# Retention and mixture of experts on one core: another order for the first two pairs of chunks

## The chip, the core and the metric

The kernel runs on one core of a Trainium2 chip. The metric is the device time of one execution in microseconds (us), lower is better; a kernel's time is the median of several executions. Times inside the kernel are read from a profile of one execution, in us from the start of its span.

## What is computed

The input is q, k and v of 4 batches, 8 heads, 768 positions and 64 channels, all float32. Each head keeps a state that decays by its own factor gamma; the output of that stage becomes the tokens of a layer with 8 experts, of which each token uses one.

```python
for t in range(S):
    state = gamma[None, :, None, None] * state + einsum('bhd,bhe->bhde', k[:, :, t], v[:, :, t])
    y[:, :, t] = scale * einsum('bhd,bhde->bhe', q[:, :, t], state)
...
x = y.transpose(0, 2, 1, 3).reshape(B * S, H * D)
logits = x @ w_gate
expert_idx = argmax(logits, axis=1)
...
    h = maximum(xe @ w1[e], 0.0)
    out[mask] = gate_w[mask, None] * (h @ w2[e])
```

## The kernel before, in words

The first stage goes over 24 chunks of 128 positions (all 8 heads of one batch at once, 6 chunks to a batch), two chunks to a turn of the loop over `k`: in turn `k`, `a` is chunk 2k and `b` is chunk 2k+1. The instructions stand in the order in which the code is written, on each engine by itself; nothing rearranges them. Later stages run the experts; the change does not touch them.

A chunk's input is one tile `qkv_t` of 128 partitions and four blocks: q and k turned (block 0 and 1, channels on the partitions), v and k as they are (blocks 2 and 3). `load(g, part)` fetches blocks of chunk g with one DMA issued on SyncE's queue (SP); all four blocks are 1,024 KB, two are 512 KB. Five such buffers go round, and `vs0`, the scaled v of chunk 0, lies in the first of them, so that the load of chunk 4 waits until chunk 0's `vs0` is used up.

For a chunk g the work is:

- `scale(g)`: v times a decay by position, into `vs` (line 250; GpSimd for all chunks but chunk 0, which VectorE does before the change).
- `scores(g)`: q times k on TensorE into two PSUM tiles `sp` (line 261), then VectorE multiplies them with the masked decay `M` into `Sb` (line 264, two instructions).
- `update(g)`: k times `vs` added into the running state `U` in PSUM (line 275), then ScalarE copies it scaled into one of three `ub` tiles (line 280, four instructions).
- `carry(g)`: the state of the chunks before, `ub` of chunk g-1, times q, into `Y` (line 291); the first chunk of a batch has none.
- `output(g)`: `Sb` times v, added into `Y` (line 302). `turn_out(g)`: VectorE multiplies `Y` with the decay `G` into `xT` (line 310).
- `gate_rows` turns a pair's output into rows and gate logits (lines 333, 317, 343).

`G` is made by one TensorE matmul `spread` from the small tile `g2` (the input `gdec`, two rows of 640) and a ScalarE copy. `cs` holds constants; its first part, which `M` needs, is loaded first. Ahead of all of this TensorE runs `WARM` matmuls of ones into the PSUM tile `warm`, which nothing reads.

Of the kernel before, what the change touches and what calls it, by code (L numbers as in the profile page):

```python
# [9 lines left out]
F32 = mybir.dt.float32  # L10
# [8 lines left out]
E, DM, F = 8, 512, 1024  # L19
N = B * S  # L20
P = 128
NP = H // 2
C = 128
# [20 lines left out]
IDS = 0x3FFF  # L44
FILLED = 160
ZROWS = 96
WARM = 12
FILL = (2, 2, 2, 2)
AHEAD = 5
BIG = 1 << 20  # L50
# [62 lines left out]
def retention_moe(ctx, tc, qkv, wts, cst, gdec, out):  # L113
    nc = tc.nc
# [44 lines left out]
    ones = gate.tile([P, P], BF16, name="ones")  # L159
# [51 lines left out]
    with ExitStack() as actx:  # L211
# [8 lines left out]
        ps_m = apool("ps_m", 1, space=PS)  # L220
# [3 lines left out]
        G = flat[:, 0:NP * C].rearrange("p (n t) -> p n t", n=NP)  # L224
# [12 lines left out]
        def load(g, part=slice(0, 4)):  # L237
            if g not in qs:
                qs[g] = ld.tile([P, 4, DM], F32, name="qkv_t", tag="ld")
            nc.sync.dma_start(out=qs[g][:, part], in_=qkv[g][:, part])  # L240
# [51 lines left out]
                                             rhs=q[half[r], p, :], start=(first and m == 0), stop=False,  # L292
                                             skip_group_check=True)

        def output(g):
            Y, Sb = Ys[g], Sbs[g]
            vp = qs[g][:, 2].rearrange("a (n d) -> a n d", n=NP)
            for m in range(2):
                for r in range(2):
                    for o in range(2):  # L300
                        p = 2 * m + o
                        nc.tensor.matmul(out=Y[half[o], r, m * C:(m + 1) * C], lhsT=vp[:, p, half[r]],  # L302
                                         rhs=Sb[:, r, p, :], start=False, stop=True, skip_group_check=True)

        def turn_out(g):
            Y = Ys[g]
# [147 lines left out]
        g2 = rawp.tile([2, DM + P], F32, name="g2", tag="raw")  # L454
        vs0 = ld.tile([P, H, D], F32, name="vs0", tag="ld")

        qs[1], qs[0] = [ld.tile([P, 4, DM], F32, name="qkv_t", tag="ld") for _ in range(2)]
        nc.sync.dma_start(out=cs[:, 0:NFIRST], in_=cst[:, 0:NFIRST])
        load(0)
        load(1, slice(0, 2))  # L460
        load(1, slice(2, 4))
        nc.sync.dma_start(out=g2, in_=gdec)
        nc.vector.memset(run, 0.0)
        nc.gpsimd.memset(meta0, 0.0)
        nc.scalar.copy(out=top, in_=run[:, 0:1])
        nc.vector.memset(wgs, 0.0)
        nc.vector.memset(zeros, 0.0)
        warm = ps_m.tile([P, 512], F32, name="warm", tag="mm")
        for i in range(WARM):
            nc.tensor.matmul(out=warm, lhsT=ones, rhs=ones.unsqueeze(1).broadcast_to([P, 4, P]), start=True, stop=True)  # L470
        load(2)
        load(3, slice(0, 2))
        load(3, slice(2, 4))
# [1 line left out]
        for r in range(2):  # L475
            nc.vector.tensor_tensor(
                out=M[:, r], in0=causal.unsqueeze(1).broadcast_to([P, NP, C]), op=ALU.mult,
                in1=cv[:, 0].rearrange("a (n t) -> a t n", t=2)[:, r].unsqueeze(2).broadcast_to([P, NP, C]))
        scale(0, nc.vector, vs0)
        scores(0)  # L480
        update(0)
        load(4)
        stages = {}
# [20 lines left out]
        for k in range(NCH // 2):  # L504
            a, b = 2 * k, 2 * k + 1
            batch, c = divmod(a, CPB)
            last = k == NCH // 2 - 1
            if k:
                scores(a)
            scores(b)  # L510
            carry(a, True)
            carry(b, c == 0)
            if last:
                xt0 = ld.tile([P, KD, EARLY], F32, name="xt0", tag="ld")
                for j, w in HALVES:
                    turn_slices(nc, xt0, xg0, j, w)
            if k - 1 in CHOSEN:
                stages["advance"]()
                if not last:
                    stages["weights"]()  # L520
            sends = list(range(*SENDS.get(k, (0, 0))))
            scale(b)
            if k not in (4, NCH // 2 - 1) and sends:
                send_x(sends.pop(0))
            if not last:
                scale(b + 1)
            if k == 10:
                send_x(sends.pop(0))
            for j, i in enumerate(SPLITS.get(k, ())):
                split(0, *divmod(i, 4), nc.gpsimd if j and k < 10 else nc.vector, 1)  # L530
            if k > 1:
                gate_rows(k, sends)
            if k == 1:
                nc.vector.tensor_tensor(out=us, in0=causal, in1=ident, op=ALU.subtract)
                nc.vector.tensor_scalar(out=run, in0=k_("ebase"), scalar1=1.0 / P, scalar2=None, op0=ALU.mult)
                for to, n in ((0, E), (E, 1)):
                    nc.vector.tensor_copy(out=wgs[:, :, to:to + n],
                                          in_=k_("gate").rearrange("p (n e) -> p n e", e=E)[:, :, 0:n])
            if k == 0:
                output(a)  # L540
            if c < CPB - 2:
                update(b)
            if not last:
                for i in sends:
                    send_x(i)
            if last:
                hidden, low, result, send, hidden_early = early_half(tc, ring[:, 4:6].rearrange("a j q m -> a j (q m)")[:, :, 0:DM],
                                            wk.tile([P, 4, EARLY], F32, name="rx0", tag="xT"),
                                            ps_1.tile([P, EARLY], F32, name="ph0", tag="U"),
                                            wp, ps_s, wparts, xhl, sidx0, meta0, out)  # L550
            if k in CHOSEN:
                stages = gating(CHOSEN[k])
                stages["choose"]()
                stages["soft"]()
            if last:

                after(EA[0:1, GROUPS[-2][0], 1:2])
                nc.gpsimd.tensor_tensor(out=xhl[:, 1], in0=xt0, in1=xhl[:, 0].bitcast(F32), op=ALU.subtract)
                for i in sends:
                    send_x(i)  # L560
            if k:
                output(a)
            output(b)
            if k == 0:
                spread = ps_m.tile([P, NP, C], F32, name="spread", tag="mm")
                nc.tensor.matmul(out=spread, lhsT=g2[:, DM:], rhs=g2[:, 0:DM], start=True, stop=True)
                nc.scalar.copy(out=G, in_=spread)
            turn_out(a)
            turn_out(b)
            if k == 1:  # L570
                gate_rows(k)
            if not last:
                update(b + 1)
            if k in CHOSEN and not last:
                stages["rank"](ps_m, "mm")
                stages["slots"]()
                if k == NCH // 2 - 2:
                    stages["weights"]()
            for g in range(2 * k + AHEAD, min(2 * k + AHEAD + 2, NCH)):
                load(g, slice(0, 4 if g % CPB < CPB - 1 else 3))  # L580
            if k == 1:
                for e in (E, E9):
                    clear(slice(e * N + FILLED, e * N + FILLED + ZROWS))
            if k in FETCHES:
                fetch(0, FETCHES[k])
            if k == 9:
                xg0 = ring[:, 2 * CPB - 2:].rearrange("a g q m -> a (g q) m")
                xhl = new_xhl(EARLY)
                load_x(xg0, E9, NJ0)
                load_meta(meta0[:, 0:2], E9, 2)  # L590
# [617 lines left out]
```

## Time and profile before

| | |
|---|---|
| time, median of 3 executions | 389.41 us (388.25 to 389.46) |
| the profiled execution | 388.81 us, of which the profile's span is 387.0 us |
| TensorE busy | 377.4 us, 98% of the span |
| VectorE, ScalarE, GpSimd busy | 258.6, 153.8, 164.1 us |
| HBM read and written | 65.07 and 15.19 MB |

A row of the timeline gives the start, how long the row's instructions took together, the engine, the line, the operation, the tile written and the tiles read, and their count; in brackets stands how long the engine had been idle and what ended that. PE is TensorE's matmul side, PEld its weight load, DVE is VectorE, ACT ScalarE, POOL GpSimd, SPq the queue of SyncE. Matmuls overlap at their ends, so the work of a row is read from its start to the next row's start, where no wait lies between. A float32 matmul of the code is two instructions in the trace.

### The profile page before, as it was taken

To read this page: it belongs to the slowest core of one execution; us is meant where nothing else is said; L and a number is where in the kernel's file an instruction comes from. 1 tells how busy PE (TensorE), PEld (TensorE's weight loads), DVE (VectorE), ACT (ScalarE), POOL (GpSimd) and SP (SyncE) were. 2 spreads that over 40 slices of the span, in tenths; PEclk is the share of its full clock that TensorE was granted. 3 is DMA by queue.
4 is the path that set the end of the run, shared out by engine and by line. 5 is a ranking of instruction groups with operands and counts; after the bars stand their busy time and mean duration, and the time that the engine had idled before them with its cause. 6 is when DMAs were issued, how large, how long until landed. Compare 5 with 4: busy or idle time off the path is not lost.

```text
span 387.0 us, 8716 instructions
## 1 busy us (share of the span) xinstructions
PE 377.4 (98%) x3279; PEld 353.3 (91%) x3279; DVE 258.6 (67%) x566; ACT 153.8 (40%) x315; POOL 164.1 (42%) x154
## 2 busy tenths in 40 slices
PE   7999999999999999899999999999999999999994
PEld 4888888888989899799999999999999999999984
DVE  4547759789878687656784777387747847776411
ACT  2335455454634455324530553155234406423200
POOL 0332755848721241001742383347317523732743
PEclk9999999999999999999999999999999999999999
DMA  7999799997358589781658357635836683530111
GB/s 274 416 382 345 275 417 420 406 383 238 141 152 209 187 278 221 244 205 30 239 167 205 101 180 193 173 132 163 226 122 197 224 205 127 183 113 5 57 42 58
DMA packets 30207, 80.65 MB, mean 208 GB/s; under 512 B 4811, under 2 KB 18767, under 8 KB 23732
## 3 DMA queue, kind: packets, MB, share of 16 engines
q1 hardware_dynamic: 24868, 66.87, 53.3%
q0 software_dynamic: 5264, 12.69, 9.1%
q8 instruction: 58, 0.95, 1.0%
q14 instruction: 17, 0.14, 0.1%
HBM read 65.07 MB, written 15.19 MB: 207 GB/s over the span
## 4 chain that ended last, share of the span: by engine, by line
PE 93%; DMA 3%; POOL 1%; SPq 1%; issue 1%; DVE 0%; POOLq 0%; DVEq 0%
PE ph L993 34%; PE py L1039 27%; PE py L1037 6%; PE sp L261 5%; PE Y L302 5%; PE xp L317 3%; DMA qkv_t<-qkv 3%; PE ph L775 3%; PE Y L291 2%; PE U L275 2%; PE L L333 2%; PE ph L915 1%; PE py L793 1%; PE lp L343 1%; POOL vs L250 1%
## 5 line engine op out<-in xcount | busy, mean ns | idle before, releaser
L733 POOL DMA_INDIRECT out<-Z,sidx x82 | 93.9, 1145 | 133.0 <-DVE Z L932 109.3
L150 DVE TENSOR_TENSOR wlo<-raw,whi 128x1024 fp32r<-128x1024 f32 (+1 forms) x67 | 75.7, 1134 | 8.2 <-ACT whi L148 7.1
L148 ACT CAST whi<-raw 128x1024 fp32r<-128x1024 f32 (+1 forms) x72 | 67.5, 952 | 1.3 <-DMA raw<-w 1.3
L1039 PE MATMUL py<-hh,whi 128*128 128x392 f32 (+4 forms) x192 | 66.3, 345 | 1.4 <-issue 1.3
L1005 ACT ACTIVATE hh<-ph 128x64 fp32r<-128x64 f32 (+7 forms) x72 | 32.3, 460 | 87.6 <-PE ph L993 86.2
L1039 PE MATMUL py<-hl,whi 128*128 128x392 f32 (+4 forms) x192 | 66.1, 344 | 0.0
L1039 PE MATMUL py<-hh,wlo 128*128 128x392 f32 (+4 forms) x192 | 66.0, 344 | 0.0
L1007 DVE SCALAR_TENSOR_TENSOR hl<-ph,hh 128x64 fp32r<-128x64 f32 (+7 forms) x72 | 36.4, 515 | 32.9 <-ACT hh L1005 32.0
L993 PE MATMUL ph<-xh,whi 128*128 128x392 f32 (+5 forms) x224 | 49.3, 342 | 0.0
L993 PE MATMUL ph<-xh,wlo 128*128 128x392 f32 (+5 forms) x224 | 49.0, 340 | 0.0
L993 PE MATMUL ph<-xl,whi 128*128 128x392 f32 (+5 forms) x224 | 49.0, 340 | 0.0
L993 PEld LDWEIGHTS ph<-xh,whi 128*128 128x128 f32 x224 | 40.3, 188 | 0.4
L993 PEld LDWEIGHTS ph<-xh,wlo 128*128 128x128 f32 x224 | 40.4, 188 | 0.2
L993 PEld LDWEIGHTS ph<-xl,whi 128*128 128x128 f32 x224 | 40.2, 188 | 0.2
L752 ACT CAST xh<-xt 128x512 fp32r<-128x512 f32 (+7 forms) x27 | 14.9, 552 | 61.6 <-DVE xt L743 61.6
L1039 PEld LDWEIGHTS py<-hh,whi 128*128 128x128 f32 x192 | 36.1, 188 | 2.2 <-issue 2.0
L1039 PEld LDWEIGHTS py<-hl,whi 128*128 128x128 f32 x192 | 36.2, 188 | 0.3
L1039 PEld LDWEIGHTS py<-hh,wlo 128*128 128x128 f32 x192 | 36.1, 188 | 0.2
L250 POOL TENSOR_TENSOR vs<-qkv_t,cs 128x512 f32<-128x512 f32 x19 | 19.8, 1044 | 36.9 <-DMA qkv_t<-qkv 31.5
L264 DVE TENSOR_TENSOR Sb<-sp,xgs 128x512 f32<-128x512 f32 x48 | 29.9, 682 | 4.4 <-PE sp L261 4.4
L733 POOL DMA_INDIRECT xs_dram<-xn,KEY x24 | 25.5, 1063 | 12.5 <-PE lp L343 4.9
L280 ACT ACTIVATE ub<-U,cs 128x64 f32<-128x64 f32 x80 | 18.5, 314 | 24.7 <-PE U L275 24.7
(169 smaller groups left out, 524.2 us busy)
## 6 DMA issues: line engine op xcount, KB each, us to landing
raw<-w SPq DMA_DIRECT2D x32, 1024.0 KB, 6.2
qkv_t<-qkv SPq DMA_DIRECT2D x18, 1024.0 KB, 9.6
qkv_t<-qkv SPq DMA_DIRECT2D x4, 768.0 KB, 6.8
xgs<-xs_dram SPq DMA_DIRECT2D x12, 211.2 KB, 4.7
qkv_t<-qkv SPq DMA_DIRECT2D x4, 512.0 KB, 7.5
xgs<-xs_dram SPq DMA_DIRECT2D x8, 227.5 KB, 4.2
out<-Z,sidx POOLq DMA_INDIRECT x82, 4.2
xs_dram<-zero SPq DMA_DIRECT2D x6, 195.0 KB, 5.7
```

What stands on the lines that cost most here:

```text
L148: nc.scalar.copy(out=hi[:, h], in_=raw[:, h])
L150: engine.tensor_tensor(out=lo[:, h], in0=raw[:, h], in1=hi[:, h].bitcast(F32), op=ALU.subtract)
L250: engine.tensor_tensor(out=vs, in0=qs[g][:, 2].rearrange("a (h d) -> a h d", d=D), in1=cv[:, c, :].unsqueeze(2).broadcast_to([P, H, D]), o ...
L261: nc.tensor.matmul(out=sps[r][:, p, :], lhsT=kt[half[r], p, :], rhs=q[half[r], p, :], start=True, stop=True)
L264: nc.vector.tensor_tensor(out=Sb[:, r], in0=sps[r], in1=M[:, r], op=ALU.mult)
L302: nc.tensor.matmul(out=Y[half[o], r, m * C:(m + 1) * C], lhsT=vp[:, p, half[r]], rhs=Sb[:, r, p, :], start=False, stop=True, skip_group_ch ...
L733: sc = tc.nc.gpsimd.indirect_dma_start(out=out, out_offset=bass.IndirectOffsetOnAxis(ap=index, axis=0), in_=rows, in_offset=None, bounds_c ...
L993: nc.tensor.matmul(out=ph[:, :w], lhsT=wparts[e, f // 4][a][:, kd, fo:fo + P], rhs=x[:, kd, :w], start=(n == 0), stop=(n == 3 * KD - 1))
L1005: nc.scalar.activation(out=to, in_=of, func=AF.Relu)
L1007: nc.vector.scalar_tensor_tensor(out=low, in0=of, scalar=0.0, in1=to.bitcast(F32), op0=ALU.max, op1=ALU.subtract)
L1037: nc.tensor.matmul(out=py[:w, :], lhsT=at, rhs=a[:, f % 4, :], **se)
L1039: nc.tensor.matmul(out=py[:, :cols], lhsT=a[:, f % 4, k * P:(k + 1) * P], rhs=x[:, :cols], **se)
```

## The change

Chunk 0 is loaded in two halves, with the small `g2` between them; 8 of the 12 matmuls of ones stay ahead and 5 others are put behind the scores of chunk 0; `output(0)` follows them, ahead of `update(0)`, and starts the accumulation in `Y`; `vs0` is made by GpSimd; `spread` and the copy into `G` stand ahead of the updates and outputs of chunk 1; in the next turn the scores of chunk 2 stand ahead of its update, and the outputs of chunk 2 ahead of the update of chunk 3.

```diff
-WARM = 12
+WARM, BETWEEN = 8, 5
...
-        def output(g):
+        def output(g, first=False):
...
-                                         rhs=Sb[:, r, p, :], start=False, stop=True, skip_group_check=True)
+                                         rhs=Sb[:, r, p, :], start=(first and m == 0), stop=True, skip_group_check=True)
...
-        load(0)
+        load(0, slice(0, 2))
+        nc.sync.dma_start(out=g2, in_=gdec)
+        load(0, slice(2, 4))
         load(1, slice(0, 2))
         load(1, slice(2, 4))
-        nc.sync.dma_start(out=g2, in_=gdec)
...
-        for i in range(WARM):
-            nc.tensor.matmul(out=warm, lhsT=ones, rhs=ones.unsqueeze(1).broadcast_to([P, 4, P]), start=True, stop=True)
+
+        def warm_up(n):
+            for i in range(n):
+                nc.tensor.matmul(out=warm, lhsT=ones, rhs=ones.unsqueeze(1).broadcast_to([P, 4, P]), start=True, stop=True)
+
+        warm_up(WARM)
...
-        scale(0, nc.vector, vs0)
+        scale(0, nc.gpsimd, vs0)
         scores(0)
+        warm_up(BETWEEN)
+        carry(0, True)
+        output(0, True)
         update(0)
         load(4)
...
+            if k == 1:
+                update(a)
             scores(b)
-            carry(a, True)
-            carry(b, c == 0)
+            if k:
+                carry(a, True)
+            carry(b, k > 0 and c == 0)
...
             if k == 0:
+                spread = ps_m.tile([P, NP, C], F32, name="spread", tag="mm")
+                nc.tensor.matmul(out=spread, lhsT=g2[:, DM:], rhs=g2[:, 0:DM], start=True, stop=True)
+                nc.scalar.copy(out=G, in_=spread)
+            if k == 1:
                 output(a)
             if c < CPB - 2:
                 update(b)
...
-            if k:
+            if k > 1:
                 output(a)
             output(b)
-            if k == 0:
-                spread = ps_m.tile([P, NP, C], F32, name="spread", tag="mm")
-                nc.tensor.matmul(out=spread, lhsT=g2[:, DM:], rhs=g2[:, 0:DM], start=True, stop=True)
-                nc.scalar.copy(out=G, in_=spread)
...
-            if not last:
+            if k and not last:
                 update(b + 1)
```

The rows below are the program's instructions on one engine in their order (line, operation, tile written, tiles read, size, count; `_124` is the tile `vs0`, `ub_120` to `ub_122` are the three `ub`). First TensorE before the change, from the scores of chunk 0 to `spread`.

```order
L261 MATMUL sp<-qkv_t 128x128 x8
L275 MATMUL U<-vs_124,qkv_t 64x64 x8
L261 MATMUL sp<-qkv_t 128x128 x8
L291 MATMUL Y<-qkv_t,ub_120 64x128 x8
L302 MATMUL Y<-Sb,qkv_t 64x128 x8
L275 MATMUL U<-vs,qkv_t 64x64 x8
L302 MATMUL Y<-Sb,qkv_t 64x128 x8
L566 MATMUL spread<-g_123 128x512
```

The same place of the changed kernel, from the scores of chunk 0 to the outputs of chunk 1; the five matmuls of ones are five such pairs of rows, of which one is shown.

```order
L261 MATMUL sp<-qkv_t 128x128 x8
L473 LDWEIGHTS ones
L473 MATMUL warm<-ones 128x512
...
L302 MATMUL Y<-Sb,qkv_t 64x128 x8
L275 MATMUL U<-vs_124,qkv_t 64x64 x8
L261 MATMUL sp<-qkv_t 128x128 x8
L291 MATMUL Y<-qkv_t,ub_120 64x128 x8
L552 MATMUL spread<-g_123 128x512
L275 MATMUL U<-vs,qkv_t 64x64 x8
L302 MATMUL Y<-Sb,qkv_t 64x128 x8
```

The outputs of chunk 0 (the first L302 row) moved from behind the carry of chunk 1 to ahead of the update of chunk 0, and `spread` moved ahead of the update and the outputs of chunk 1. Next, TensorE before the change in the turn of chunks 2 and 3, up to the logits of the first pair.

```order
L275 MATMUL U<-vs,qkv_t 64x64 x8
L261 MATMUL sp<-qkv_t 128x128 x16
L291 MATMUL Y<-qkv_t,ub_121 64x128 x8
L291 MATMUL Y<-qkv_t,ub_122 64x128 x8
L275 MATMUL U<-vs,qkv_t 64x64 x8
L302 MATMUL Y<-Sb,qkv_t 64x128 x16
L333 MATMUL L<-xT,xgs 32x256 x4
```

The same place of the changed kernel.

```order
L261 MATMUL sp<-qkv_t 128x128 x8
L275 MATMUL U<-vs,qkv_t 64x64 x8
L261 MATMUL sp<-qkv_t 128x128 x8
L291 MATMUL Y<-qkv_t,ub_121 64x128 x8
L291 MATMUL Y<-qkv_t,ub_122 64x128 x8
L302 MATMUL Y<-Sb,qkv_t 64x128 x8
L275 MATMUL U<-vs,qkv_t 64x64 x8
L302 MATMUL Y<-Sb,qkv_t 64x128 x8
L333 MATMUL L<-xT,xgs 32x256 x4
```

The update of chunk 2 now has the scores of chunk 2 ahead of it, and the update of chunk 3 has the outputs of chunk 2 ahead of it. Last, the DMA issues at the head of SyncE's queue before the change.

```order
L458 DMA cs<-cst 128x200
L240 DMA qkv_t<-qkv 128x2048
L240 DMA qkv_t<-qkv 128x1024 x2
L462 DMA g_123<-gdec 2x640
L240 DMA qkv_t<-qkv 128x2048
L240 DMA qkv_t<-qkv 128x1024 x2
L474 DMA cs<-cst 128x310
```

The same head in the changed kernel.

```order
L458 DMA cs<-cst 128x200
L240 DMA qkv_t<-qkv 128x1024
L460 DMA g_123<-gdec 2x640
L240 DMA qkv_t<-qkv 128x1024 x3
L240 DMA qkv_t<-qkv 128x2048
L240 DMA qkv_t<-qkv 128x1024 x2
L479 DMA cs<-cst 128x310
```

There is one issue more, and `g2` stands ahead of the second half of chunk 0 and of both halves of chunk 1.

## Rows read from the trace of the kernel before

**Rows 1.** The profile's page: its first line, and the chain that ended last.

```profile
span 387.0 us, 8716 instructions
...
PE 93%; DMA 3%; POOL 1%; SPq 1%; issue 1%; DVE 0%; POOLq 0%; DVEq 0%
```

**Rows 2.** TensorE's timeline, from the start to the update of chunk 4.

```profile
1.08 4.47 PE L470 MATMUL warm<-ones 128*128 128x512 bf16 x12 [1.08 <-DVE ones L160]
6.19 1.16 PE L261 MATMUL sp<-qkv_t 64*128 64x128 f32 x16 [0.64 <-DMA qkv_t<-qkv]
7.28 0.69 PE L275 MATMUL U<-vs,qkv_t 128*64 128x64 f32 x16
8.35 1.16 PE L261 MATMUL sp<-qkv_t 64*128 64x128 f32 x16 [0.38 <-DMA qkv_t<-qkv]
...
10.04 1.09 PE L302 MATMUL Y<-Sb,qkv_t 128*64 128x128 f32 x16
10.96 0.63 PE L275 MATMUL U<-vs,qkv_t 128*64 128x64 f32 x16
11.43 1.04 PE L302 MATMUL Y<-Sb,qkv_t 128*64 128x128 f32 x16
12.40 1.12 PE L566 MATMUL spread<-g 2*128 2x512 f32 x2
...
16.05 1.10 PE L291 MATMUL Y<-qkv_t,ub 64*64 64x128 f32 x32
17.29 0.69 PE L275 MATMUL U<-vs,qkv_t 128*64 128x64 f32 x16
17.81 1.92 PE L302 MATMUL Y<-Sb,qkv_t 128*64 128x128 f32 x32
19.66 0.64 PE L333 MATMUL L<-xT,xgs 128*32 128x256 f32 x8
...
21.47 0.69 PE L275 MATMUL U<-vs,qkv_t 128*64 128x64 f32 x16
```

**Rows 3.** Stages: busy time of PE, PEld, DVE, ACT, POOL; granted clock, DMA share, GB/s.

```profile
0.00:4.00 4.00, 2.92 (x7) 1.04 (x8) 2.23 (x7) 1.47 (x2) 0.31 (x5) 1.00 0.54 136
4.00:6.00 2.00, 1.55 (x6) 0.50 (x4) 0.11 (x1) 0.00 (x0) 0.00 (x0) 1.00 0.96 391
6.00:8.00 2.00, 1.78 (x32) 1.52 (x32) 1.31 (x3) 0.00 (x0) 0.00 (x0) 1.00 0.90 295
10.00:14.00 4.00, 4.00 (x70) 3.03 (x66) 0.83 (x2) 1.37 (x5) 1.84 (x2) 1.00 1.01 412
20.00:115.00 95.00, 94.79 (x1536) 82.78 (x1528) 73.21 (x201) 48.07 (x141) 53.18 (x54) 1.00 0.83 314
```

**Rows 4.** The timeline of GpSimd: the scaled v of chunks 3 and 4.

```profile
16.19 1.04 POOL L250 TENSOR_TENSOR vs<-qkv_t,cs 128x512 f32<-128x512 f32 x1 [2.98 <-DMA qkv_t<-qkv]
19.19 1.04 POOL L250 TENSOR_TENSOR vs<-qkv_t,cs 128x512 f32<-128x512 f32 x1 [1.95 <-DMA qkv_t<-qkv]
```

**Rows 5.** TensorE's weight loads: the last matmuls of ones, and the update of chunk 3.

```profile
4.04 0.15 PEld L470 LDWEIGHTS <-ones 128*128 128x128 bf16 x1 [0.27 <-issue]
4.47 0.58 PEld L470 LDWEIGHTS <-ones 128*128 128x128 bf16 x3 [0.28 <-issue]
...
17.29 0.55 PEld L275 LDWEIGHTS U<-vs,qkv_t 128*64 128x64 f32 x16 [0.38 <-POOL vs L250]
```

**Rows 6.** The timeline of VectorE: the scaled v and the masked scores of chunk 0.

```profile
6.17 0.69 DVE L250 TENSOR_TENSOR vs<-qkv_t,cs 128x512 f32<-128x512 f32 x1 [2.06 <-DMA qkv_t<-qkv]
7.38 1.29 DVE L264 TENSOR_TENSOR Sb<-sp,xgs 128x512 f32<-128x512 f32 x2 [0.52 <-PE sp L261]
```

**Rows 7.** The timeline of ScalarE: the copies of the first state into `ub`.

```profile
8.01 0.93 ACT L280 ACTIVATE ub<-U,cs 128x64 f32<-128x64 f32 x4 [5.77 <-PE U L275]
```

**Rows 8.** SyncE's queue: the issues of chunks 0 and 1, and of `g2`.

```profile
1.22 1.37 SPq L240 DMA_DIRECT2D qkv_t<-qkv  x3
2.63 0.63 SPq L462 DMA_DIRECT2D g<-gdec  x1
```

## The prediction

> **What bounds the kernel now.** I read the page first. Its chain is 93% TensorE and 3% DMA [rows 1]: once TensorE has data it sets the end. The windows say where it lacks work: from 20 to 115 us it is busy 94.79 of 95 us [rows 3], so whatever it finishes sooner before 20 us moves the rest up, unless a transfer stops it. The timeline of the first 20 us shows its gaps: it starts on chunk 0 at 6.19 after 0.64 us idle, waits 0.38 us for chunk 1 until 8.35, and works on with one more stop, at the update of chunk 3 [rows 2]. There the weight load stood 0.38 us for the scaled v [rows 5]. The carries ahead of it ran from 16.05 for 1.10 us, to 17.15 at most, and the update began at 17.29 [rows 2]; of the two I count 0.20 us as lost on the matmul side, nearer the matmuls' own row. That v was made by GpSimd from 16.19 to 17.23, at once when chunk 3's last half had landed [rows 4]. So three arrivals bind: chunk 0 at 6.2, chunk 1's first half at 8.35, chunk 3's last half at 16.2.
>
> **Chunk 0 in halves.** The scores need q and k turned, which is the first half. By the windows 4 x 136 = 544 kB had moved by 4.0 us, and 391 kB per us after it [rows 3]. The constants (128 x 200 x 4 B = 102 kB) and the whole of chunk 0 (1,049 kB) are 1,151 kB, reached at 4.0 + 607/391 = 5.55; the consumer started at 6.19, 0.64 later. Constants and half a chunk are 627 kB, reached at 4.21. With the same lag the scores start at 4.85. The nearest other lag is chunk 1's first half: 1,675 kB are reached at 7.18 (1,326 kB by 6.0, then 295 per us) and it was used at 8.35, 1.17 later; that gives 5.38 as the late bound. The early bound is 4.52, when the first eight matmuls of ones are over: 1.08 plus eight spacings of 0.43 [rows 2, 5]. I take 4.85, since it is the same transfer.
>
> **Up to the scores of chunk 1.** From a start s: scores 1.09 us (6.19 to 7.28) [rows 2]. Five matmuls of ones at the spacing of the last before, (0.58 - 0.15)/2 = 0.215 [rows 5], 1.08. They lie in a wait: VectorE began the masked scores 1.19 after the scores did and took 1.29 for two [rows 6], so the second stands at s + 2.48; without the five, TensorE would idle. The outputs start at s + 2.17, use the first half of `Sb` for a quarter of their 0.92 us (10.04 to 10.96) [rows 2], wait 0.1 and end at s + 3.19. The update of chunk 0 takes 0.52 (17.29 to 17.81) [rows 2]: s + 3.71, which is 8.56. Chunk 1's first half was there at 8.35, so its scores begin at 8.56, 0.21 later than before, with the outputs of chunk 0 already done.
>
> **What lies beside that.** GpSimd takes 1.04 for v of chunk 0 where VectorE took 0.69 [rows 4, 6]. The second half lands at about 5.56 + 0.64 = 6.2, so v is ready at 7.24; the update wants it at 8.04. Cover 0.8 us; past it each 0.1 us costs 0.1. The issue of `g2`, 0.63 us, now stands ahead of that half, and there is one issue more, 1.37/3 = 0.46 [rows 8]. Chunks 1 to 3 are thus issued up to 1.1 us later (the first half of chunk 1), but until 4.2 us the engines have the first half to move and then hold a backlog (their share is 0.96 from 4 to 6 and 1.01 from 10 to 14 [rows 3]). I cost both at nothing; were the backlog to run dry, 1.1 us would come on top of 8.35. The copy into `ub`, 0.93 [rows 7], fits under the scores of chunk 1, 1.09. The load of chunk 4 waits for `vs0`, about 0.6 us longer, behind the same backlog.
>
> **From chunk 1 to the logits.** Before, TensorE worked from 8.35 to 17.09 (17.29 less the 0.20), 8.74 us. Without the outputs of chunk 0 that is 7.82; the other moves change the order only. From 8.56 this ends at 16.38. `spread` done sooner lets VectorE turn out the first pair sooner, so the masked scores of chunk 2 stand more than 1 us before their use. Now the outputs of chunk 2 come first, 0.925 (half of 17.81 to 19.66) [rows 2]: 17.30. Chunk 3's v was ready at 17.23, so its update does not wait: 17.82, then the outputs of chunk 3: 18.75. Before it was 19.66. The sum is -0.92 for the outputs moved into the head, -0.20 for the stall, +0.21 for the later scores: **-0.91 us**. The next arrival is close as well: with chunk 3's v landing as before, the update cannot begin ahead of 17.29, which caps the gain at 0.93. Only if chunk 3 lands sooner could a start at 4.52 give 1.12. After that the update of chunk 4 moves from 21.47 to 20.56 [rows 2], and its v is ready at 20.23 [rows 4]: 0.33 us are left there.
>
> So the profiled execution's 388.81 us become 387.90 (span 387.0 to 386.1). It stands 0.6 below the median of the runs shown, 389.41, by which the sum would be 388.50; I forecast **388.2**, the middle.
>
> **Rivals.** *The clock is not up (slower).* The first eight matmuls of ones stood 0.43 us apart, 512 columns at 1.2 GHz, and from 4.47 on 0.215, at 2.4 GHz [rows 2, 5]; the granted column reads 1.00 in that window too [rows 3], so the rise is read from the spacing. Twelve ones at 0.43 would last to 6.2: before, TensorE was covered until chunk 0 came, even with a late rise. Now the ones end at 4.52 and 0.3 us of nothing follow. If the rise then comes only two ones after the scores, they cost 1.09 more and the ones 0.43: the scores of chunk 1 at 10.08, and the balance is -0.92 - 0.20 + 1.73 = +0.61, 389.4. It decides once more than 0.91 us is lost; were all up to the outputs at half speed, +3.1 would give 391.0. For it speaks that the ones end just where the rise was seen. Against it: before, 0.64 us of idle right after the rise did not undo it. The Trainium skill (TensorE: Matmul & The Clock Gate, Part 1) says that the monitor behind this runs on its own and does not start anew with a kernel, so that the moment of the rise differs between runs. By that rule this rival comes true in some executions only; the single trace here cannot show it.
>
> *Half loads flow slower.* From 6 to 8 us, when chunk 1's two halves flowed, the rate was 295 kB per us against 391 just before; against it, from 10 to 14 us, with chunk 3's halves among them, 412 [rows 3]. If chunk 0 from 4.0 on went at 295, the scores would start at 4.92 and chunk 1's first half be used at 9.02, 0.67 later: gain 0.45. If chunk 3 is late by as much, its cap leaves 0.26: 388.55. The Trainium skill (DMA: Bandwidth & Descriptors, Bandwidth: Measured) advises to batch DMAs to 1 MiB or more; by that rule the split costs rate. The row from 10 to 14 does not bear it out here.
>
> *The halves land together.* If q and k of chunk 0 come no sooner than 6.19, the scores of chunk 1 start at 9.90: -0.92 - 0.20 + 1.55 = +0.43, 389.24. Nothing in the rows speaks for it but the lags, which differ by half a us.
>
> *The lead is lost later.* If chunk 4 lands 0.33 us or more later, or a later stage waits on something timed by DMA, up to all 0.91 is taken back: 388.81. Against it stands the unbroken 20 to 115 us.
>
> **Chances.** Forecast (gain 0.38 to 1.12): 0.62. Clock: 0.13. Slow halves: 0.12. Landing together: 0.06. Lost later: 0.07. I take 0.3%, 1.17 us, as what a measurement can tell from no change; the three runs shown spread over 1.2. No mechanism here reaches 1.17, but the forecast's 0.91 plus that scatter passes it in about 4 of 10 of its 0.62: faster 0.25. Slower beyond 1.17 is the worse half of the clock rival and a little scatter: 0.08. Same 0.67. The range reaches down to the gain of 1.12 with half the scatter, 387.1, and up to the clock's and the joint landing's 389.4.
>
> **What the profile after would show.** Scores of chunk 0 at 4.85 (4.52 to 5.4) at 1.09 us for sixteen; the five ones 0.215 apart; outputs of chunk 0 done by 8.1; scores of chunk 1 near 8.56, without a wait for DMA; the update of chunk 3 at 17.3 with hardly a wait; the first logits at 18.75; the update of chunk 4 at 20.56. I would be wrong if the ones behind the scores stand 0.43 apart, if the scores start after 5.4, if chunk 3's v is ready at another time than 17.2, or if the logits come 0.9 us sooner and the end doesn't.

## Result and the profile after

The changed kernel takes **391.69 us** (median of 6 executions, 390.88 to 392.06) against 389.44 (388.25 to 390.57) for the kernel before on the same chip: a ratio of 1.0055 [1.0035, 1.0076], slower by 2.1 us where 0.9 less was forecast. The profiled execution took 391.22, its span 389.4, 2.4 more than before. A ratio, here and below, is estimated from the single executions and not from the two medians; it leaves out those over 1.5% above the fastest of their kernel (two of twelve in g2_late_w8, one of twelve in warm8_only, and one of the kernel before on two of the chips).

TensorE's timeline of the changed kernel, from the ones ahead to the first logits, answers to [rows 2].

```profile
1.08 3.60 PE L473 MATMUL warm<-ones 128*128 128x512 bf16 x8 [1.08 <-DVE ones L160]
5.76 2.08 PE L261 MATMUL sp<-qkv_t 64*128 64x128 f32 x16 [1.08 <-DMA qkv_t<-qkv]
7.77 2.32 PE L473 MATMUL warm<-ones 128*128 128x512 bf16 x5
10.02 1.09 PE L302 MATMUL Y<-Sb,qkv_t 128*64 128x128 f32 x16
10.94 0.63 PE L275 MATMUL U<-vs,qkv_t 128*64 128x64 f32 x16
11.51 1.16 PE L261 MATMUL sp<-qkv_t 64*128 64x128 f32 x16
...
15.74 1.16 PE L261 MATMUL sp<-qkv_t 64*128 64x128 f32 x16
16.83 0.69 PE L275 MATMUL U<-vs,qkv_t 128*64 128x64 f32 x16
17.44 1.16 PE L261 MATMUL sp<-qkv_t 64*128 64x128 f32 x16
18.54 1.10 PE L291 MATMUL Y<-qkv_t,ub 64*64 64x128 f32 x32
19.57 1.09 PE L302 MATMUL Y<-Sb,qkv_t 128*64 128x128 f32 x16
20.49 0.63 PE L275 MATMUL U<-vs,qkv_t 128*64 128x64 f32 x16
...
21.93 0.64 PE L333 MATMUL L<-xT,xgs 128*32 128x256 f32 x8
```

The scores of chunk 0 waited 1.08 us for the load and took 2.01 us to the next row's start, not 1.09: half speed. The scores of chunk 1 start at 11.51, not 8.56. That difference of 2.95 is 0.91 (start at 5.76, not 4.85), 0.92 (scores at half speed), 1.07 (ones, wait and outputs in 3.17, not 2.10) and 0.05 (update). Behind it only 0.23 is added: the logits come 10.42 us after the scores of chunk 1, forecast 10.19. The update of chunk 3 waits for nothing, and the first logits stand at 21.93, 2.27 later than before. This is nearly all of the 2.4.

The weight loads of the five ones, which answer to [rows 5], give the clock.

```profile
8.18 0.15 PEld L473 LDWEIGHTS <-ones 128*128 128x128 bf16 x1 [0.28 <-issue]
8.60 0.15 PEld L473 LDWEIGHTS <-ones 128*128 128x128 bf16 x1 [0.27 <-issue]
```

They stand 0.43 us apart, as 512 columns at 1.2 GHz would, more than three us after the moment at which the kernel before was at 2.4 GHz. In GpSimd's timeline, the scaled v of chunks 0 and 3 [rows 4, 6]:

```profile
9.25 1.04 POOL L250 TENSOR_TENSOR vs<-qkv_t,cs 128x512 f32<-128x512 f32 x1 [8.39 <-DMA qkv_t<-qkv]
...
17.01 1.04 POOL L250 TENSOR_TENSOR vs<-qkv_t,cs 128x512 f32<-128x512 f32 x1 [1.52 <-DMA qkv_t<-qkv]
```

GpSimd could start on the second half of chunk 0 at 9.25, forecast 6.2: 3 us later, where the prediction had 0.8 us of cover. Chunk 3's v was ready at 18.05, forecast 17.23. SyncE's issues [rows 8] and the windows [rows 3]:

```profile
1.68 0.34 SPq L460 DMA_DIRECT2D g<-gdec  x1
2.06 1.29 SPq L240 DMA_DIRECT2D qkv_t<-qkv  x3
3.40 2.77 SPq L240 DMA_DIRECT2D qkv_t<-qkv  x3
```

```profile
0.00:4.00 4.00, 2.92 (x7) 1.04 (x8) 2.20 (x7) 1.47 (x2) 0.31 (x5) 1.00 0.50 104
4.00:6.00 2.00, 0.92 (x4) 0.24 (x4) 0.14 (x1) 0.00 (x0) 0.00 (x0) 1.00 0.95 324
6.00:8.00 2.00, 2.00 (x17) 1.68 (x18) 0.13 (x1) 0.00 (x0) 0.00 (x0) 1.00 0.94 285
...
20.00:115.00 95.00, 94.79 (x1572) 83.02 (x1567) 74.62 (x203) 48.49 (x144) 54.09 (x54) 1.00 0.83 315
```

The three loads behind `g2` (the second half of chunk 0, both halves of chunk 1) take 0.43 us each to issue, no longer than the 0.46 before; only the next three, chunks 2 and 3, take 0.92 each. So the second half was issued by 2.4 us and still came 3 us late. Up to 8.0 us 104 x 4 + 324 x 2 + 285 x 2 = 1,634 kB have moved, before 1,916. The engines are as busy as before (0.95, 0.94): they move less while busy. From 20 to 115 us TensorE is busy 94.79 us again, so in this execution what is lost ahead of it stays lost.

### The profile page after: what moved, and what is told of

It reads as the page before. It is cut to its first block, busy times and chain, and to the rows that moved or that the text cites. A ratio compares the mean times of both kernels' runs of the same rounds, so it can differ in the third digit from the quotient of the medians.

```text
span 389.4 us, 8719 instructions
## 1 busy us (share of the span) xinstructions
PE 379.7 (97%) x3280; PEld 354.3 (91%) x3280; DVE 260.2 (67%) x565; ACT 153.8 (39%) x315; POOL 165.3 (42%) x155
## 4 chain that ended last, share of the span: by engine, by line
PE 90%; DMA 4%; SPq 1%; issue 1%; POOL 1%; DVE 1%; ACT 1%; POOLq 0%; DVEq 0%
PE ph L1004 31%; PE py L1050 27%; PE sp L261 6%; PE Y L302 5%; PE py L1048 5%; PE xp L317 3%; PE Y L291 3%; PE U L275 3%; PE ph L786 2%; PE L L333 2%; DMA xgs<-xs_dram 2%; PE ph L926 1%; DMA xs_dram<-xgs 1%; DMA qkv_t<-qkv 1%; SPq L188 1%
## 5 line engine op out<-in xcount | busy, mean ns | idle before, releaser
L250 POOL TENSOR_TENSOR vs<-qkv_t,cs 128x512 f32<-128x512 f32 x20 | 20.9, 1044 | 36.1 <-DMA qkv_t<-qkv 33.6
```

Of the source, the lines that this page charges most:

```text
L250: engine.tensor_tensor(out=vs, in0=qs[g][:, 2].rearrange("a (h d) -> a h d", d=D), in1=cv[:, c, :].unsqueeze(2).broadcast_to([P, H, D]), o ...
```

## Experiments

The theory after this result (D in the first expectations): the halves flow slowly at the head, and `g2` between them makes it worse. Its rival (C): too few ones ahead, so the clock is late. Each ratio is to the kernel before on the same chip, with 9 to 12 executions of the experiment and 23 to 35 of before; the experiments ran on five chips, so two of them are compared by their ratios. One execution of each was profiled.

**warm12**, the change with twelve ones ahead:

```diff
-WARM, BETWEEN = 8, 5
+WARM, BETWEEN = 12, 5
```

> The changed kernel with twelve matmuls of ones ahead instead of eight; the five behind the scores stay. Theory C (the clock): the scores of chunk 0 and the five ones ran at 1.2 GHz because eight ones and then a gap of 1.1 us did not bring the clock up, and that is the loss; covered by twelve, the scores take 1.09 us instead of 2.01, the ones 0.215 apart instead of 0.43, and the time falls by about 2 us, to 389.7. Theory D (the data): the second half of chunk 0 and chunk 1 land later in the changed kernel (v of chunk 0 used at 9.25, chunk 1 used after 10.6), so the outputs of chunk 0 cannot start before 9.1 and the scores of chunk 1 not before 10.85 instead of 11.51: only 0.7 us are won back, to 391.0.

392.28 us, 1.0067 [1.0033, 1.0101]. TensorE's timeline:

```profile
6.12 1.16 PE L261 MATMUL sp<-qkv_t 64*128 64x128 f32 x16 [0.30 <-DMA qkv_t<-qkv]
7.22 1.25 PE L473 MATMUL warm<-ones 128*128 128x512 bf16 x5
9.91 1.09 PE L302 MATMUL Y<-Sb,qkv_t 128*64 128x128 f32 x16 [1.45 <-DMA qkv_t<-qkv]
```

The scores run at full speed, yet the outputs wait 1.45 us for v and the logits come at 22.06. In this execution the loads bind as soon as the clock doesn't, and the ratio is no better than with eight ones; C alone falls.

**whole0**, twelve ones, chunk 0 in one load and `g2` behind chunk 1, the rest as changed:

```diff
-        load(0, slice(0, 2))
-        nc.sync.dma_start(out=g2, in_=gdec)
-        load(0, slice(2, 4))
+        load(0)
         load(1, slice(0, 2))
         load(1, slice(2, 4))
+        nc.sync.dma_start(out=g2, in_=gdec)
```

> The changed kernel with twelve ones ahead, chunk 0 loaded whole, and the small decay tile loaded after chunk 1 as before the change; all else as changed. Theory D: the data arrive as before the change (chunk 0 at 6.2, chunk 1's first half at 8.35, chunk 3's last at about 16.2); scores of chunk 0 6.2 to 7.3, ones, outputs and update of chunk 0 to 9.9, scores of chunk 1 at 9.9, the first logits 0.4 us later than before the change: 389.9. Theory C alone: the same as with the halves and twelve ones, since loading plays no part: 389.7.

390.90 us, 1.0044 [1.0014, 1.0075]. Two rows of TensorE's timeline:

```profile
6.09 1.16 PE L261 MATMUL sp<-qkv_t 64*128 64x128 f32 x16 [0.19 <-DMA qkv_t<-qkv]
...
9.90 1.16 PE L261 MATMUL sp<-qkv_t 64*128 64x128 f32 x16
```

The step between the two takes 3.81 us, forecast 3.71, and the logits come at 20.33, 0.67 late. By the ratio the time is 1.7 us longer (0.5 to 2.9), which need not be more than that. This one execution is longer by more: its span is 390.9, 3.9 above the one before, so 3.2 of it lie behind the first logits.

**split0_only**, before with `load(0)` as two halves:

> The kernel before with one edit: chunk 0 loaded in two halves (the decay tile stays behind chunk 1). Theory D, halves at fault: the rate falls in the first 8 us, chunk 1's first half is used near 10.5 instead of 8.35, time 390.5 to 391.7. Theory D with the small decay tile between the halves at fault: nothing is lost here, 389.4. Theory C: nothing is lost, 389.4.

389.20 us, 1.0011 [0.9985, 1.0038]. Scores of chunk 0 at 6.31, VectorE's scaling of v at 7.51, scores of chunk 1 at 9.38, logits at 20.48. Here all twelve ones ran at 1.2 GHz and lasted as long, but the half itself landed only at 6.2, 5.0 us after its issue at 1.23: no sooner than a whole chunk.

**warm8_only**, before with `WARM = 8`:

> The kernel before with one edit: eight ones instead of twelve. Theory C: after 4.7 TensorE has nothing until 6.2, so the scores and the update of chunk 0 and most of the scores of chunk 1 run at 1.2 GHz (16 scores in 2.0 us, not 1.09); the scores of chunk 1 end near 10.9 instead of 9.44: 390.8. Theory D: nothing changes, 389.4.

390.83 us, 1.0031 [1.0004, 1.0058]. In the profiled execution the eight ones ran at half speed to their end (3.59 us for eight), yet the scores, after a wait, at full, and the logits stand at 19.73:

```profile
6.16 1.16 PE L261 MATMUL sp<-qkv_t 64*128 64x128 f32 x16 [1.49 <-DMA qkv_t<-qkv]
7.25 0.69 PE L275 MATMUL U<-vs,qkv_t 128*64 128x64 f32 x16
```

The longer median would fit executions in which it did not; no trace shows one.

**g2_late**, warm12 with `g2` behind chunk 1:

```diff
         load(0, slice(0, 2))
-        nc.sync.dma_start(out=g2, in_=gdec)
         load(0, slice(2, 4))
         load(1, slice(0, 2))
         load(1, slice(2, 4))
+        nc.sync.dma_start(out=g2, in_=gdec)
```

> The changed kernel with twelve ones ahead, chunk 0 still in halves, but the small decay tile loaded behind chunk 1 as before the change. Theory D1 (the two-row load between the halves holds up two of the transfer engines): chunk 0's second half and chunk 1 come as they do with the split alone (v of chunk 0 by 7.5, chunk 1's first half used at 9.4), the outputs of chunk 0 start by 8.7 without a wait for DMA, the scores of chunk 1 near 10.1 and the first logits near 20.5 instead of 22.0: about 1.5 us won back. Theory D2 (the halves alone make the data late): as with the decay tile between, outputs of chunk 0 at 9.1 to 9.9 after a wait for DMA, logits at 22.0.

390.24 us, 1.0021 [0.9995, 1.0046]. TensorE's and GpSimd's timelines:

```profile
5.49 1.16 PE L261 MATMUL sp<-qkv_t 64*128 64x128 f32 x16
6.58 1.25 PE L473 MATMUL warm<-ones 128*128 128x512 bf16 x5
7.76 1.14 PE L302 MATMUL Y<-Sb,qkv_t 128*64 128x128 f32 x16
9.29 1.16 PE L261 MATMUL sp<-qkv_t 64*128 64x128 f32 x16
```

```profile
6.91 1.04 POOL L250 TENSOR_TENSOR vs<-qkv_t,cs 128x512 f32<-128x512 f32 x1 [6.04 <-DMA qkv_t<-qkv]
```

v starts at 6.91 instead of 9.92, and the logits come at 19.72 instead of 22.06 in warm12: between these two executions 2.3 us for the place of a load of 5 kB.

**g2_front**, before with `g2` ahead of all loads of chunks, and **g2_after0**, before with `g2` between the whole chunk 0 and chunk 1:

> The kernel before with one edit: the small decay tile is loaded first, ahead of chunk 0, which stays whole. Theory D1: two transfer engines fall behind and every load after it lands late: scores of chunk 0 near 7 or later instead of 6.19, of chunk 1 after 9.5 instead of 8.35, logits 1 us later than 19.66. Theory D2: only its issue counts, 0.4 us or so: scores of chunk 0 at 6.5, of chunk 1 at 8.7, logits at 19.9.

> The kernel before with one edit: the small decay tile is loaded between the whole chunk 0 and the first half of chunk 1. Theory D1a (a two-row load among loads in 4 KB rows holds some transfer engines up): chunk 1's first half is used later than 9.5 and the engines' landings of one load spread by more than 1.5 us; logits after 20.8. Theory D1b (it does so only at the very head of the queue, ahead of chunk 0's second half): chunk 1 used at 8.4 to 8.7, logits at 19.7 to 20.0.

389.86 us, 1.0016 [0.9989, 1.0043], and 389.27, 1.0002 [0.9976, 1.0027]; logits at 20.29 and 19.50. So the small load does no measurable harm to the time ahead of a whole chunk or behind it, though the first interval leaves room for 0.4%: in g2_front the scores of chunk 0 start at 6.91, later than in any other profile.

**whole1**, before with chunk 1 as one load:

```diff
-        load(1, slice(0, 2))
-        load(1, slice(2, 4))
+        load(1)
```

> The kernel before with one edit: chunk 1 loaded whole instead of in halves. Theory H (rows of 4 KB are slow in the first 8 us, rows of 8 KB not): the rate from 6 to 8 us rises from 295 to about 390 kB per us; chunk 1, all of it, is used near 9.0 (its first half was used at 8.35), v of chunk 2 comes near 11.6 instead of 12.17. Theory T (these two microseconds are slow whatever flows): the rate stays near 290, chunk 1 is used at 9.7, v of chunk 2 still at 12.17. The time moves little by either, -0.2 to +0.5 us.

389.06 us, 0.9997 [0.9972, 1.0022]. One of its windows:

```profile
6.00:8.00 2.00, 1.62 (x32) 1.50 (x32) 1.12 (x2) 0.00 (x0) 0.00 (x0) 1.00 1.01 426
```

From 6 to 8 us the rate is 426 kB per us, where [rows 3] had 295: the halves made that dip. It is 422 in tail_whole1, and 262 to 336 in all ten profiles with chunk 0 whole and chunk 1 in halves. It gave no time: from 10 to 14 us the rate is then 359, before 412.

**tail_only**, before with `spread` sooner and the new order of chunks 2 and 3, nothing else:

> The kernel before with the later part of the change alone: the decay spread and its copy ahead of the outputs of the first pair, scores of chunk 2 ahead of its update, outputs of chunk 2 ahead of the update of chunk 3; loads, ones, v of chunk 0 and the outputs of chunk 0 as before. All theories: the update of chunk 3 no longer stalls, logits at 19.4 to 19.5 instead of 19.66, time 0.2 us less, within the noise. If this part itself costs, as a wait of the carries for VectorE, the logits come after 19.9.

389.14 us, 0.9989 [0.9965, 1.0013]. The stall at chunk 3's update is gone (it starts at 18.56, right behind the outputs of chunk 2), logits at 20.00, 11.30 after the scores of chunk 1 as before (11.31): neutral.

**loads_only**, before with the change's loads (halves, `g2` between) and nothing else:

> The kernel before with the change's order of loads alone: chunk 0 in two halves with the small decay tile between them; twelve ones, VectorE for v of chunk 0, and the old order on TensorE. Theory D1: this alone makes the data late; v of chunk 0 is not there before 9.0, the scores of chunk 1 start after 10.6 instead of 8.35, the first logits come at 21.5 to 22.3 instead of 19.66, time about 2 us above the kernel before. If the late data need the rest of the change too: logits at 20.5, as with the split alone.

390.32 us, 1.0037 [1.0012, 1.0063]. Rows of TensorE, of VectorE, and one window:

```profile
5.34 1.16 PE L261 MATMUL sp<-qkv_t 64*128 64x128 f32 x16
8.95 0.69 PE L275 MATMUL U<-vs,qkv_t 128*64 128x64 f32 x16 [2.44 <-DVE vs L250]
10.22 1.28 PE L261 MATMUL sp<-qkv_t 64*128 64x128 f32 x16 [0.58 <-DMA qkv_t<-qkv]
```

```profile
8.21 0.69 DVE L250 TENSOR_TENSOR vs<-qkv_t,cs 128x512 f32<-128x512 f32 x1 [4.04 <-DMA qkv_t<-qkv]
```

```profile
10.00:14.00 4.00, 3.78 (x46) 3.23 (x48) 1.39 (x3) 0.61 (x3) 1.04 (x1) 0.64 1.00 414
```

The order of loads by itself costs 0.37%, of 0.55 for the whole change; the two are known to 0.25 and 0.2. The first half came early (5.34), the second at 8.2. TensorE then stood idle for 2.44 us, and the granted clock of the stretch behind it reads 0.64. The late v costs twice.

**g2_late_w8**, g2_late with `WARM, BETWEEN = 8, 5`, and **after_again**, the changed kernel itself on the same chip:

> The changed kernel with the small decay tile loaded behind chunk 1, and eight ones ahead as changed: it differs by four ones from the run with that tile late and twelve ones, in which data bound nothing between the scores of chunk 0 and those of chunk 1 (5.49 to 9.29). Theory C: the scores of chunk 0 take 2.0 us and the five ones 0.43 each, the scores of chunk 1 start near 11.2, logits near 21.7, 2 us later than 19.72. If eight ones bring the clock up in this execution, as they did in the kernel before with eight: logits at 19.7.

> The changed kernel as it is, once more, beside the others on one chip. Theory D1: v of chunk 0 again not used before 9.0, the scores of chunk 1 not before 10.8, logits at 21.3 or later whatever the clock does. Theory C alone: if the scores of chunk 0 take 1.09 us this time, logits near 20 and about 2 us less than in the first profile.

390.93 us, 1.0031 [1.0002, 1.0060], and 391.52, 1.0051 [1.0021, 1.0081]. In g2_late_w8 the clock was up behind eight ones; the scores start at 5.29, v at 6.69, the scores of chunk 1 at 9.10, and the logits stand at 19.53, 0.13 sooner than before. The gain at the head is there in this execution, and the ratio shows none. Rows of TensorE's timeline in the changed kernel's second profile, first from the head, then the two longest waits of the expert stage; behind these the longest of that stage in the kernel before:

```profile
5.61 1.16 PE L261 MATMUL sp<-qkv_t 64*128 64x128 f32 x16 [0.94 <-DMA qkv_t<-qkv]
6.71 1.25 PE L473 MATMUL warm<-ones 128*128 128x512 bf16 x5
7.89 1.14 PE L302 MATMUL Y<-Sb,qkv_t 128*64 128x128 f32 x16
...
9.51 1.16 PE L261 MATMUL sp<-qkv_t 64*128 64x128 f32 x16
```

```profile
160.65 0.45 PE L1050 MATMUL py<-hh,whi 128*128 128x392 f32 x1 [0.98 <-issue]
204.03 0.46 PE L1050 MATMUL py<-hh,whi 128*128 128x422 f32 x1 [1.61 <-DVE Z L938]
```

```profile
161.02 0.45 PE L1039 MATMUL py<-hh,whi 128*128 128x392 f32 x1 [1.26 <-issue]
```

Same kernel, other loss: here the clock is up, v starts at 7.59 and the logits at 19.93 are 0.27 late, but the span, 389.7, is as long as the first one's. The rest lies in the expert stage: its waits over 0.1 us come to 3.79 us, in the kernel before to 1.64. Both wait near 161 us; the wait at 204 is the main difference. One of 1.24 to 1.82 us from 202 to 206 us stands in eight of the twenty profiles, two of them with the old head (split0_only 1.44, g2_after0 1.46). A single profile thus doesn't give the mean loss, and whether such waits belong to the head was the next question.

**before_again**, the kernel before against itself:

> The kernel before, unchanged, timed against itself. Its ratio should be 1.000 with an interval that holds 1 (1.0025 at most to either side). The gaps of TensorE in the expert stage (from the last logits to its end, 283.25 us in the one profile of before) are either chance: then this execution may as well show 284 to 286; or they belong to the changed head: then it shows 282.7 to 284.4, as the other kernels with the old head did. If the ratio lies outside 1 by 0.3%, my other differences of 0.2 to 0.4% prove little.

389.19 us, 0.9986 [0.9960, 1.0013].

**head_only**, before with the new work of chunk 0 alone, its loads whole, twelve ones ahead:

```diff
...
-        scale(0, nc.vector, vs0)
+        scale(0, nc.gpsimd, vs0)
         scores(0)
+        for i in range(5):
+            nc.tensor.matmul(out=warm, lhsT=ones, rhs=ones.unsqueeze(1).broadcast_to([P, 4, P]), start=True, stop=True)
+        carry(0, True)
+        output(0, True)
...
```

> The kernel before with its loads and its twelve ones, and of the change only what concerns chunk 0's work: v on GpSimd, five ones behind its scores, its outputs ahead of its update. Scores of chunk 0 near 6.2, scores of chunk 1 at 9.9 (3.71 later), first logits at 20.1 to 20.4 (0.5 to 0.7 after before). Theory A, that the loss is what the first 20 us show and the late gaps are chance: 389.7 at a before of 389.1, ratio 1.0015 (0.999 to 1.003). Theory B, that another head also costs gaps in the expert stage: ratio 1.004 or more, like chunk 0 whole (1.0044), and from the last logits to TensorE's end 285 to 286.5 us.

391.16 us, 1.0063 [1.0034, 1.0093]. Its timeline begins so:

```profile
1.08 5.30 PE L470 MATMUL warm<-ones 128*128 128x512 bf16 x12 [1.08 <-DVE ones L160]
6.45 1.45 PE L261 MATMUL sp<-qkv_t 64*128 64x128 f32 x16
```

Here even twelve ones ran at 1.2 GHz to their end, and the five behind the scores at 2.4 (1.18 us from 7.83 to 9.01). The logits come at 20.93, 1.27 late, and from the last logits to TensorE's end it is 283.34 us, as before (283.25). In three of its twelve executions the mean granted clock of the span was 0.993, in 2 of the 34 compared of before that low. Neither theory of the expectation holds: the ratio is B's (the two medians alone would give 1.0040), the trace without late waits A's.

**whole0_no5**, whole0 without the five ones (`WARM, BETWEEN = 12, 0`), and **tail_whole1**, tail_only and whole1 together:

> Chunk 0 whole and everything else of the change, without the five ones behind the scores. The outputs of chunk 0 start with the first masked scores and end 0.46 us behind the second (start of scores + 2.94), so the scores of chunk 1 come near 9.65 and the logits near 20.1. Theory A: ratio 1.001 to 1.002. Theory C, that the five ones cost more than their 0.25 us (they keep the array at work where it would have rested, and a later fall of the granted clock pays for it): ratio below 1.000, since without them nothing is left of the loss. Theory B: 1.004 again.

> The kernel before with the parts of the change that did no harm (spread sooner, the order of chunks 2 and 3) and chunk 1 in one load instead of two. If the two add as their ratios did alone (0.9989 and 0.9997): 0.9986, 388.5 at a before of 389.1. A gain of 0.3% or more needs the logits 1.2 us sooner, at 18.5, for which the first 20 us leave no room: rate 426 kB per us from 6 to 8 us, scores of chunk 1 near 8.7, logits near 19.7 without a stall at the update of chunk 3.

389.81 us, 1.0015 [0.9989, 1.0041], and 389.70, 1.0005 [0.9980, 1.0030]. The first raised the suspicion that the five ones cost time; the second, the version that the harmless parts point to, gains nothing.

**g2_late_no5** and **head_no5**, g2_late and head_only without the five ones:

> The change with all twelve ones ahead, g2 behind chunk 1, and no ones behind the scores of chunk 0. Without them the outputs of chunk 0 end about 0.25 us sooner, so the scores of chunk 1 come 3.45 to 3.5 us after those of chunk 0. Theory D, that the five ones cost over 1 us in the timed executions, of which only 0.25 is their place in the chain: ratio 0.9985 (0.996 to 1.001), against 1.0021 with them. Theory E, that they cost their 0.25 us alone: 1.0015, and the loss lies in what else the head does.

> The same question on the old loads: v of chunk 0 on GpSimd and the outputs of chunk 0 ahead of its update, without the five ones. Scores of chunk 0 near 6.2, scores of chunk 1 near 9.65, first logits near 20.1. Theory D: ratio 1.001 to 1.003, against 1.0063 with the five. Theory E: 1.0055.

389.56 us, 1.0019 [0.9991, 1.0047], and 389.81, 1.0013 [0.9991, 1.0036]. TensorE's timeline of g2_late_no5:

```profile
5.68 1.16 PE L261 MATMUL sp<-qkv_t 64*128 64x128 f32 x16
7.62 0.44 PE L302 MATMUL Y<-Sb,qkv_t 128*64 128x128 f32 x4 [0.78 <-DVE Sb L264]
8.21 0.88 PE L302 MATMUL Y<-Sb,qkv_t 128*64 128x128 f32 x12 [0.16 <-DVE Sb L264]
9.48 1.16 PE L261 MATMUL sp<-qkv_t 64*128 64x128 f32 x16
```

Without the ones TensorE waits 0.78 and 0.16 us for VectorE, and the scores of chunk 1 come 3.80 us after those of chunk 0, as with them (3.80 in g2_late). Expected had been 3.5: at full clock the ones are free in this chain. Over the three pairs that differ by the five ones alone, the ratio falls by 0.0029, 0.0050 and 0.0002 without them. The mean is 0.0027, and with the half widths added as squares it is known to 0.0022: 1.1 us (0.2 to 1.9). Only head_only's pair shows it by itself, and one shows nothing; without the pair that raised the suspicion the other two give 0.0026, known to 0.0027, so this cost is likely and not shown. By the medians the three are 0.0041, 0.0025 and 0.0023.

Done alike, the three pairs with `g2` between the halves and without that (warm12 and g2_late, after_again and g2_late_w8, loads_only and split0_only) give 0.0046, 0.0020, 0.0026: mean 0.0031, known to 0.0023, 1.2 us (0.3 to 2.1); by the medians 0.0051, 0.0015 and 0.0024. With the times of v this is the better founded of the two.

The third suspect, eight ones ahead in place of twelve (warm8_only against before, g2_late_w8 and g2_late, after_again and warm12), gives 0.0031, 0.0010 and -0.0016: mean 0.0008, known to 0.0022, so no mean cost is shown for it.

## Why the prediction was wrong

**The step that failed: chunk 0 in halves, and its neighbours "costed at nothing".** The scores were to start at 4.85 because half a chunk was taken to flow at the rate of a whole one, with the lag of a whole one behind it. The two signs of being wrong that were named for this came: a start after 5.4, and ones 0.43 apart. In the eight profiles with halves the scores start at 5.29 to 6.31, on average 5.7 (5.76 and 5.61 in the changed kernel), at most about 0.1 us after the half landed; with a whole chunk, in the eleven others that don't have `g2` ahead of it, at 6.09 to 6.68, on average 6.3. The halving gains 0.6 us, not 1.34. Up to the start of the scores the windows read, in the changed kernel and before:

```profile
0.00:5.76 5.76, 3.60 (x8) 1.04 (x9) 2.34 (x7) 1.47 (x2) 0.31 (x5) 1.00 0.63 171
```

```profile
0.00:6.19 6.19, 4.47 (x13) 1.54 (x13) 2.36 (x8) 1.47 (x2) 0.31 (x5) 1.00 0.70 225
```

So 985 kB had moved by 5.76, 358 more than the 627 that the scores need; before, 1,393 by 6.19, 242 more than 1,151. Bytes of the loads behind move before the first is complete, and the fixed lag of 0.64 stood for them. In the changed kernel 627 kB are reached at 4.65 (416 by 4.0, then 324 per us), not 4.21, and the scores follow 1.11 later, not 0.64: of the 0.91 about half is the slower flow and half the longer lag.

The rival "half loads flow slower" thus had the first of these and priced it at 0.07 us of start, at 295 kB per us from 4.0 on; what was missed is the second, and the rate ahead of 4.0 (104 against 136). I dismissed it by the row from 10 to 14 us (412 kB per us), which isn't the head: from 6 to 8 us the rate with chunk 1's halves was 295 before, 285 after (there with the second half of chunk 0), and whole1 raised the same two us to 426. The Trainium skill (DMA: Bandwidth & Descriptors, Bandwidth: Measured) advises loads of 1 MiB; at the head the traces agree with it, from 10 to 14 us (415 in the changed kernel, loads of both sizes) they don't.

**The cover for v did not hold.** `g2` ahead of the second half was costed at nothing, with a cover of 0.8 us named. In the four profiles with it between the halves, v's scaling starts at 9.25, 9.92, 8.21 and 7.59; in the four with halves and without it there (g2_late, g2_late_no5, g2_late_w8, split0_only) at 6.91, 7.00, 6.69 and 7.51. From 4 to 6 us the first four move 263 to 324 kB per us, the others 340 to 377. The backlog, which the prediction feared for, did not run dry: the engines' share in the changed kernel is 0.95 and 0.94 from 4 to 8 us. With the cover gone, the loads by themselves cost 0.37%.

**The clock rival came true in one profile of the changed kernel and not in the other**, with 2.0 us between the two in scores and ones (2.01 + 2.25 against 1.10 + 1.18). The Trainium skill (TensorE: Matmul & The Clock Gate, Part 1) says that the moment of the rise differs between runs; here it does, by the spacing of the ones: by 4.5 us in the kernel before, not yet by 6.2 in head_only, not yet by 9.0 in the changed kernel. The prediction had priced this: all up to the outputs at half speed would give 391.0. That this lies near the 391.22 of the profiled execution is luck, since the load made 0.91 of its delay, and the second profile took 391.50 with the clock up. The cost of 1.1 us for the five ones over all executions would fit a late clock, in which they take 0.43 us each in the path, but the trace of such a loss is one (the changed kernel's first), and warm12 shows that loads would have held it up as far.

**The terms of the sum.** From the scores of chunk 0 to those of chunk 1: 3.80 at full clock, forecast 3.71. From there to the logits: 10.43 in whole0, g2_late and g2_late_no5, forecast 10.19, before 11.31: the moved outputs and the stall give 0.88, not 1.12. The scores of chunks 2 and 3, now in two blocks, take 1.09 and 1.10 us; in one block they took 1.98 (14.08 to 16.06 in before_again), which is 0.21 of it. So the change breaks even where s + 3.80 + 10.43 = 19.66, at a start of s = 5.43, and at 5.7 loses 0.3. In g2_late_no5, freed of both faults, the logits come 0.25 late (s = 5.68); in g2_late_w8, at s = 5.29, 0.13 early. The interval of the ratio of g2_late_no5, from 0.9991 up, leaves out the forecast gain of 0.23%.

**Right** were the way through (20 to 115 us pass on what the head loses), the end of the stall at chunk 3's update, `spread`, and GpSimd's 1.04 us for v.

**What stays open.** The two parts, 1.2 us for `g2` between the halves and a likely 1.1 for the five ones, are 2.3 together, against a measured 2.1; each is known only to about 1 us, and g2_late_no5, which has neither, still reads 1.0019. So that the loads cost time is shown, and how the 2.1 divide is not. Why two rows of 2.5 kB between two halves slow the second half is not shown, nor why ones that ran at full clock in every profile but one should cost anything. Waits in the expert stage vary: from the last logits to TensorE's end, 282.7 to 285.0 us in ten profiles with the old work of chunk 0, 282.9 to 286.9 in ten with the new. The means are 283.5 and 284.6 and the ranges overlap; that the new head brings more of them was neither shown nor excluded.

## What to carry to other kernels

Take the rate of a transfer from the stretch in which it will run: a window with the same shape later in the kernel said nothing of the first 8 us. Do not count a load as complete when its own bytes could have moved: here 240 to 360 kB of the loads behind it had moved as well. A load split to start sooner has to be paid by the second half too, so put nothing between the halves and name what waits for the second. Work moved into a head that waits for data gains only if the head's start moves as well: write down the start at which it breaks even (here 5.43) before trusting the gain, and take several executions, since one profile of the same kernel put 2.3 us of loss into the head and the next put it elsewhere.

## What the hardware showed unasked

The granted clock fell inside a running kernel. It read 0.64 from 10 to 14 us in loads_only, after TensorE's 2.44 us of idle, and 0.57 in the second of these windows of warm12, behind a stretch in which TensorE had been busy 4.18 of 6 us, with one wait of 1.82 up to 205.79. The third row is whole0's, behind a wait of 1.77 us at the same place, which ended at 204.96: there the clock stayed at 1.00.

```profile
200.00:206.00 6.00, 4.18 (x22) 3.75 (x21) 5.03 (x10) 1.57 (x2) 1.94 (x2) 1.00 0.53 199
206.00:210.00 4.00, 4.00 (x14) 3.80 (x14) 1.31 (x3) 0.62 (x1) 0.97 (x1) 0.57 0.97 197
```

```profile
206.00:210.00 4.00, 4.00 (x22) 3.91 (x22) 0.80 (x2) 0.49 (x1) 0.46 (x1) 1.00 1.18 227
```

At the head, 0.64 us of idle in the kernel before [rows 2] and 1.62 in g2_front had no such effect. The clock also rose across a wait: in warm8_only, g2_late_w8 and the changed kernel's second profile the eight ones ran at half speed to their end (3.55 to 3.59 us), and after 1.49, 0.66 and 0.94 us of idle the scores took 1.09 to 1.10; in the changed kernel's first profile, after 1.08 us, they took 2.01.
